# A branch that is never taken on GpSimd, and fifteen small loads among the large ones

## The chip, the cores and the metric

The kernel runs on one NeuronCore of a Trainium2 chip. A core has a matrix engine (TensorE, PE in the profile), a vector engine (VectorE, DVE), a scalar engine (ScalarE, ACT), a general engine (GpSimd, POOL) and a synchronisation engine (SyncE, SP). Each has its own instruction stream; they meet through semaphores. Sixteen DMA engines move data between device memory (HBM) and the on-chip memory SBUF, which has 128 partitions; TensorE writes into PSUM. SP and ACT put transfers on queues of their own (q1 and q10 in the profile's rows), and the engines' instructions are brought in by a further queue (q8). The metric is device time in microseconds of one execution.

## The reference

The reference is one step of a decoder for one token: grouped-query attention over a cached context, a SwiGLU feed-forward block, and a scalar gate that mixes the two.

```python
def reference(A_x, A_k_cache, A_v_cache, A_wq, A_wo, B_x, B_w_gate, B_w_up, B_w_down, gate_w):
    x = A_x                                                   # [1, 1, 512]
    g = sigmoid((x * gate_w).sum(-1, keepdims=True))
    q = (x @ A_wq)  -> 32 heads of 128                        # wq [512, 4096]
    k, v: caches [1, 8, 32768, 128], each used by 4 heads
    p = softmax(q @ k^T * 128 ** -0.5)
    a = (p @ v) -> [1, 1, 4096] @ A_wo                        # wo [4096, 512]
    b = (silu(x @ B_w_gate) * (x @ B_w_up)) @ B_w_down        # F = 1792
    return g * a + (1 - g) * b
```

All tensors are bf16. The two caches are 64 MiB each, so nearly everything that is moved is K and V: 8 groups of 8 MiB of K and 8 MiB of V.

## The kernel before, in words

**Loads.** SP issues nearly all loads, in this order: wq (4 MiB), w_gate and w_up (1.75 MiB each), then K of group 0 in two halves of 4 MiB, K of group 1 in two halves, V of group 0, and from then on in turn K of group g and V of group g-1, each as one load of 8 MiB in which each of the 128 partitions receives 64 KiB. Last come V of group 7, w_down, two small remainders of w_down, and wo in five pieces. `load_k` and `load_v` do the issuing. SBUF holds five pages of 32 KiB per partition (`page`), so SP waits before most of these loads until a page is free: a K load waits until half of the preceding group's K has been transposed (`sem_fill`, L311; for the second half of group 1, L320), a V load until the V products of an earlier group are done (`sem_v_free`, L335), V of group 0 until the feed-forward projections are done (`sem_pe_h`). SP runs in program order, so what stands behind a waiting load waits with it.

**TensorE.** Its program is one loop of two turns with two tests, so that the code of the end stands ahead of the code of the start. The start (`emit_start`) makes an identity matrix from a row of indices (`r_row`, L476), turns x into a column (L482), computes the q projection (L497) when wq has landed, brings q into place (L522), and computes the gate and up projections (L535) when those weights have landed, followed by small steps (L553, L566). Then a loop over the 8 groups: K is transposed on TensorE in 16 units (L371) into PSUM, VectorE copies each unit to SBUF (`ktT`, L765), TensorE multiplies it by q (L383). The maximum, the exponentials (ACT, L633) and the products with V (L440) of a group follow, the V products one group later than the K work. The end (`emit_end`) adds the last group's V products, the down projection (L235) and the product with wo (L235, L246).

**GpSimd.** POOL's program is short. It fills `ones_f` and `ones_bf` (L278, L279), builds `r_row` by doubling (L280 to L290: seven additions and one negation), and then only passes on semaphore counts of the K loads, and late in the kernel clears the small tile for the remainders of w_down (L301). TensorE's very first matmul waits for `ones_f`, `ones_bf` and `r_row`; VectorE's work at the start and all of TensorE's program stand behind that matmul.

**Tiles.** `pad` is a tile that nothing uses; its size comes from `PAD`. It stands ahead of `page` in SBUF, so its size moves `page` and the tiles behind it.

Of the kernel before, what the change touches and what calls it, by code (L numbers as in the profile page):

```python
# [8 lines left out]
BF16 = mybir.dt.bfloat16  # L9
# [3 lines left out]
def bass_gated_mix__gqa_block_cached__swiglu_ffn__decode_kernel(  # L13
# [61 lines left out]
    NPG = 5  # L75
    assert G % 2 == 0
    PAD = 768

    XH, XE, XQ, FX = 2, 4, 4, 4
    XP = XE * XQ  # L80
# [6 lines left out]
    with ExitStack() as es:  # L87
        def S_(name):
            return es.enter_context(nc.semaphore(name))
# [10 lines left out]
        sem_ld_wd = S_("s_ld_wd")  # L100
        sem_ld_wx = S_("s_ld_wx")
        sem_wz = S_("s_wz")
        sem_ones = S_("s_ones")
        sem_dc = S_("s_dc")
        sem_pz = S_("s_pz")
# [42 lines left out]
        def T(name, shape, dt):  # L148
            return es.enter_context(nc.sbuf_tensor(name, shape, dt))
# [6 lines left out]
        ones_f = T("ones_f", [128, 128], FP32)  # L156
# [11 lines left out]
        tX = T("tX", [XS, FX], BF16)  # L168
        pad = T("pad", [128, PAD // 2], BF16)
        page = T("page", [128, NPG, PAGE], BF16)  # L170
# [14 lines left out]
        O2a = T("O2a", [128, WOJ], BF16)  # L185
        O2 = T("O2", [128, WOJ], BF16)
        res_row = T("res_row", [128, 128], BF16)

        def P(name, shape, dt):
            return es.enter_context(nc.psum_tensor(name, shape, dt))  # L190
# [78 lines left out]
        def emit_store(eng, half, rows):  # L269
            eng.dma_start(  # L270
                out[0, 0, 256 * half : 256 * (half + 1)].rearrange("(c n) -> c n", c=2),
                rows[31 + 64 * half : 33 + 64 * half, :],
            ).then_inc(sem_out, 16)

        with nc.Block("main") as block:
            @block.gpsimd
            def _(pool):
                pool.memset(ones_f[:, :], 1.0).then_inc(sem_ones, 1)  # L278
                pool.memset(ones_bf[:, :], 1.0).then_inc(sem_ones, 1)  # L279
                pool.memset(r_row[:, 0, 0:1], 0.0).then_inc(sem_r, 1)  # L280
                n, k = 1, 1
                while n < 128:
                    pool.wait_ge(sem_r, k)
                    pool.tensor_scalar(
                        r_row[:, 0, n : 2 * n], r_row[:, 0, 0:n], float(n), None, op0=ALU.add
                    ).then_inc(sem_r, 1)
                    n *= 2
                    k += 1
                pool.wait_ge(sem_r, k)
                pool.tensor_scalar(  # L290
                    r_row[:, 1, :], r_row[:, 0, :], -1.0, None, op0=ALU.mult
                ).then_inc(sem_r, 1)
                for g in range(1, G):
                    pool.wait_ge(sem_k[1], 16 * g)
                    if g > 1:
                        pool.wait_ge(sem_k[0], 16 * (g + 1))
                    else:
                        pool.wait_ge(sem_k1, 16)
                    pool.sem_inc(sem_k[1], 16)
                pool.wait_ge(sem_fill, UPG * G)  # L300
                pool.memset(wz, 0.0).then_inc(sem_wz, 1)  # L301

            @block.sync
            def _(sp):
                def load_k(g):
                    lo = PG_A if g % 2 else PG_B
                    dst = page[:, lo : lo + NB, :].rearrange("p b (r d) -> p b r d", d=DH)
                    src = A_k_cache[0, g, :, :].rearrange("(p b r) d -> p b r d", b=NB, r=R)
                    if g > 1:
                        sp.wait_ge(sem_fill, UPG * (g - 1) + UPP)  # L310
                        sp.dma_start(  # L311
                            dst.rearrange("p b r d -> p (b r d)"),
                            src.rearrange("p b r d -> p (b r d)"),
                        ).then_inc(sem_k[0], 16)
                        return
                    for b in range(NB):
                        first = lo + b == PG_B
                        if g and first:
                            sp.wait_ge(sem_fill, UPP)
                        sp.dma_start(dst[:, b, :, :], src[:, b, :, :]).then_inc(  # L320
                            sem_k[0] if first else sem_k1 if g else sem_k[1], 16
                        )

                def load_v(g):
                    src = A_v_cache[0, g, :, :].rearrange("(p b r) d -> p b r d", b=NB, r=R)
                    if g == G - 1:
                        lo, sem = PG_L, sem_vl
                        sp.wait_ge(sem_fill, UPG * g + UPP)
                    else:
                        lo, sem = PG_V, sem_v  # L330
                        if g:
                            sp.wait_ge(sem_v_free, STEP * (g + 1))
                        else:
                            sp.wait_ge(sem_pe_h, 1)
                    sp.dma_start(  # L335
                        page[:, lo : lo + NB, :].rearrange("p b n -> p (b n)"),
                        src.rearrange("p b r d -> p (b r d)"),
                    ).then_inc(sem, 16)

                sp.dma_start(wq_v, A_wq.rearrange("(p c) n -> p c n", c=KC)).then_inc(sem_q, 16)  # L340
                for w, src in enumerate((B_w_gate, B_w_up)):
                    sp.dma_start(
                        wgu[:, w, :, :], src.rearrange("(p c) f -> p c f", c=KC)
                    ).then_inc(sem_f, 16)
                load_k(0)
                for g in range(1, G):
                    load_k(g)
                    load_v(g - 1)
                load_v(G - 1)
                sp.dma_start(  # L350
                    wd[:, :, :], B_w_down[0:FR, :].rearrange("(p j) n -> p j n", j=FM)
                ).then_inc(sem_ld_wd, 16)
                sp.wait_ge(sem_wz, 1)
                rest = B_w_down[FR:F, :].rearrange(
                    "(h q e i) n -> h e q (i n)", h=XH, q=XQ, e=XE
                )
                for h in range(XH):
                    sp.dma_start(wx[h], rest[h]).then_inc(sem_ld_wx, 16)
                sp.wait_ge(sem_v_free, STEP * G)
                src = A_wo.rearrange("(p j) n -> p j n", j=WOJ)  # L360
                for k, s in enumerate(sem_wo):
                    a, b = WO_CUTS[k], WO_CUTS[k + 1]
                    sp.dma_start(wo_v[:, a:b, :], src[:, a:b, :]).then_inc(s, 16)  # L363
# [445 lines left out]
        pe, act, dve, sp = nc.tensor, nc.scalar, nc.vector, nc.sync  # L809
# [9 lines left out]
        for half, eng in enumerate((sp, act)):  # L819
            eng.wait_ge(sem_dve_row, 1)  # L820
            emit_store(eng, half, res_row)
        sp.wait_ge(sem_out, 32)


# [26 lines left out]
```

## Time and profile before

| | |
|---|---|
| median of 3 runs | 349.12 us (348.97 to 349.3) |
| the profiled execution | 349.16 us |
| its span, first to last instruction | 347.8 us |
| moved from HBM | 148.11 MB, 426 GB/s over the span |
| busy share of PE, DVE, ACT, POOL | 75%, 54%, 10%, 1% |
| mean granted TensorE clock | 0.851 |
| POOL instructions | 16, 4.6 us in all |

Engines: PE is TensorE's matrix work and PEld its weight loads, DVE VectorE, ACT ScalarE, POOL GpSimd, SP SyncE; a trailing q (SPq, ACTq) is an engine's instruction sequencer. A row of the timeline gives start, duration, engine, line, operation, what is written and read, how often, and in brackets the idle time before and what ended it. A row of the DMA queues gives queue, packets, MB and the time of its packets as a share of 16 engines over the span or the window asked for. A row "DMA packets" counts the packets of a window and how many were smaller than 512 B, 2 KB and 8 KB (each count holds the ones before). A row of the stages gives start and end, then for PE, PEld, DVE, ACT and POOL the busy time and the number of instructions, the granted clock, the DMA share and GB/s.

### The profile page before, as it was taken

The page shows a single profiled execution, that of the slowest core. Times are in us where ns is not written, and L with a number is a line of the kernel's source. Part 1 is how long each engine was busy: PE and PEld are TensorE (multiplying, and loading weights), DVE is VectorE, ACT ScalarE, POOL GpSimd, SP SyncE. Part 2 cuts the span into 40 slices and gives each one's busy share as a digit, 9 for nine tenths or more (in the row PEclk, how much of TensorE's full clock was granted, in tenths as well). Part 3 has the DMA queues.
Part 4 walks back from the last instruction along what each step waited for, and adds up shares of the span by engine and source line. Part 5 has one row for each costly group of instructions (what it writes and reads, how often), then busy time and mean ns, then how long its engine had stood idle before and what let it go on. Part 6 is the DMA issues. An engine that isn't in the chain of part 4 may idle for free.

```text
span 347.8 us, 8869 instructions
## 1 busy us (share of the span) xinstructions
PE 260.8 (75%) x3925; PEld 220.6 (63%) x3925; DVE 186.6 (54%) x232; ACT 33.4 (10%) x143; POOL 4.6 (1%) x16
## 2 busy tenths in 40 slices
PE   1354995999749982999459982999469972999475
PEld 1124994998449941997259942996269842996232
DVE  3144995698119931697129921895149820895101
ACT  1002000300130003000300003000400012000400
POOL 3000000000000000000000000000000000002000
PEclk9996999699659987699959985898869985898669
DMA  8999999999999999999999999999999999999996
GB/s 322 419 459 426 420 422 458 469 414 437 414 430 475 415 437 415 437 467 415 437 407 445 467 414 437 407 452 460 414 437 407 452 460 415 437 407 452 406 418 261
DMA packets 3946, 148.21 MB, mean 426 GB/s; under 512 B 450, under 2 KB 580, under 8 KB 868
## 3 DMA queue, kind: packets, MB, share of 16 engines
q1 hardware_dynamic: 3932, 148.11, 98.7%
q8 instruction: 6, 0.10, 0.1%
q10 hardware_dynamic: 8, 0.00, 0.0%
HBM read 148.11 MB, written 0.00 MB: 426 GB/s over the span
## 4 chain that ended last, share of the span: by engine, by line
DMA 64%; PE 33%; DVE 2%; issue 1%; SPq 1%; ACT 0%; DVEq 0%
DMA page<-in_A_k_cache_dram 52%; PE pst L371 24%; DMA page<-in_B_w_up_dram 6%; DMA page<-in_A_wo_dram 6%; PE ps_sc L383 5%; PE ps_o L440 2%; PE pst L535 1%; DVE ktT L722 1%; DVE ktT L765 0%; SPq L363 0%; PE ps_m L553 0%; PE ps_m L566 0%; DVE ktT L712 0%; DVE ktT L710 0%; PE ps_sc L246 0%
## 5 line engine op out<-in xcount | busy, mean ns | idle before, releaser
L765 DVE COPY ktT<-pst 128x2048 bf16<-128x2048 bf16 x128 | 153.3, 1221 | 64.6 <-PE pst L371 60.4
L371 PE MATMUL pst<-ident_f,page 128*128 128x128 f32 x1024 | 147.2, 299 | 39.5 <-DMA page<-in_A_k_cache_dram 38.2
L371 PEld LDWEIGHTS pst<-ident_f,page 128*128 128x128 f32 x1024 | 126.0, 154 | 43.9 <-DMA page<-in_A_k_cache_dram 38.8
L383 PE MATMUL ps_sc<-qcur,ktT 128*128 128x8 bf16 x2048 | 64.1, 166 | 6.3 <-DVE ktT L765 6.3
L383 PEld LDWEIGHTS ps_sc<-qcur,ktT 128*128 128x128 bf16 x2048 | 63.8, 97 | 8.0 <-DVE ktT L765 7.1
L440 PE MATMUL ps_o<-page,ET 128*16 128x512 bf16 x512 | 39.4, 477 | 5.5 <-DMA page<-in_A_v_cache_dram 5.5
L440 PEld LDWEIGHTS ps_o<-page,ET 128*16 128x16 bf16 x512 | 15.0, 107 | 26.1 <-issue 18.8
L633 ACT ACTIVATE ET<-ps_sc,nbias 128x128 bf16 x64 | 23.9, 555 | 49.9 <-DVE nbias L791 49.9
L626 ACT ACTIVATE acc<-ps_o 128x512 f32<-128x512 f32 x8 | 4.8, 597 | 223.8 <-PE ps_o L440 218.9
L783 DVE TENSOR_REDUCE gm<-ps_m 4x1 f32<-4x128 f32 x8 | 2.2, 279 | 40.6 <-PE ps_m L420 40.6
L633 ACT ACTIVATION_READ_ACCUMULATOR ET<-ps_sc,nbias 128x1 f32 x64 | 18.3, 285 | 0.0
L773 DVE TENSOR_REDUCE pmaxf<-ps_sc 128x4 f32<-128x512 f32 x16 | 11.0, 686 | 8.4 <-PE ps_sc L383 8.4
L497 PE MATMUL pst<-page,xT 128*1 128x512 bf16 x32 | 3.6, 627 | 8.9 <-DMA page<-in_A_wq_dram 8.9
L461 PE MATMUL ps_m<-sel,acc 128*128 128x4 f32 x64 | 8.4, 255 | 1.8 <-ACT acc L626 1.6
L461 PEld LDWEIGHTS ps_m<-sel,acc 128*128 128x128 f32 x64 | 7.7, 191 | 2.5 <-ACT acc L626 2.2
L424 PE MATMUL ps_m<-diag,ones_f 4*128 4x4 f32 x16 | 3.8, 306 | 6.8 <-DVE diag L787 6.8
L424 PEld LDWEIGHTS ps_m<-diag,ones_f 4*128 4x128 f32 x16 | 3.3, 259 | 8.4 <-issue 8.4
L750 DVE RECIPROCAL rS<-ps_m 128x4 f32<-128x4 f32 x9 | 1.6, 182 | 12.2 <-PE ps_m L461 12.2
L497 PEld LDWEIGHTS pst<-page,xT 128*1 128x1 bf16 x32 | 0.9, 115 | 10.7 <-issue 10.7
L685 DVE CAST ktT<-pst 128x1024 bf16<-128x1024 f32 x2 | 2.4, 1220 | 8.2 <-PE pst L497 8.2
L452 PEld LDWEIGHTS ps_m<-esum,ones_f 128*128 128x128 f32 x32 | 4.2, 190 | 3.5 <-issue 3.5
L301 POOL MEMSET page<- 48x2048 bf16 x1 | 1.8, 1798 | 311.7 <-PE pst L371 311.7
(76 smaller groups left out, 54.6 us busy)
## 6 DMA issues: line engine op xcount, KB each, us to landing
page<-in_A_k_cache_dram SPq DMA_DIRECT2D x4, 4096.0 KB, 34.9
page<-in_A_wq_dram SPq DMA_DIRECT2D x1, 4096.0 KB, 13.4
page<-in_A_wo_dram SPq DMA_DIRECT2D x1, 2048.0 KB, 17.4
page<-in_B_w_gate_dram SPq DMA_DIRECT2D x1, 1792.0 KB, 17.2
page<-in_B_w_up_dram SPq DMA_DIRECT2D x1, 1792.0 KB, 21.0
wd<-in_B_w_down_dram SPq DMA_DIRECT2D x1, 1664.0 KB, 30.3
page<-in_A_wo_dram SPq DMA_DIRECT2D x1, 1152.0 KB, 19.8
page<-in_A_wo_dram SPq DMA_DIRECT2D x1, 512.0 KB, 20.6
```

The costliest lines, as they stand in the source:

```text
L371: ins = pe.transpose(pst[u % NST][:, k * 128 : (k + 1) * 128], kv[:, n * 128 : (n + 1) * 128], ident_f[:, :],)
L383: ins = pe.matmul(ps_sc[b][:, col : col + 2 * HPG], kt[:, k, e, :], qcur[:, e, :], start=(e == 0), stop=(e == 1),)
L424: pe.matmul(ps_m[:, M_B0 : M_B0 + HPG], ones_f[0:HPG, :], diag[:, :], start=True, stop=True,).then_inc(sem_b, STEP)
L440: ins = pe.matmul(ps_o[32 * c : 32 * c + RQ * HPG, :], ET[:, n : n + RQ, :].rearrange("p n h -> p (n h)"), v[:, k * RQ : (k + 1) * RQ, :], ...
L452: pe.matmul(ps_m[:, M_S0 : M_S0 + HPG], ones_f[:, :], esum[:, b, :], start=(b == 0), stop=(b == NB - 1),)
L461: ins = pe.matmul(ps_m[:, M_P0 : M_P0 + HPG], acc[:, q, :], sel4[:, q * HPG : (q + 1) * HPG], start=(q == 0), stop=(q == RQ - 1),)
L497: ins = pe.matmul(pst[0][32 * k : 32 * k + 1, t * QN : (t + 1) * QN], xT[:, c : c + 1], wq_v[:, c, n : n + QN], start=(c == 0), stop=(c == ...
L535: ins = pe.matmul(pst[1][32 * k : 32 * k + 1, w * 512 : w * 512 + FS], xT[:, c : c + 1], wgu[:, w, c, k * FS : (k + 1) * FS], start=(c == ...
L626: act.activation(part, ps_o[:, :], ACT.Copy).then_inc(sem_acc, STEP)
L633: act.activation(ET[:, b * R : (b + 1) * R, h], sc[:, h, bass.ds(bank, R)], ACT.Exp, bias=nbias[:, h : h + 1], scale=SCALE, accum_out=esum ...
L765: dve.tensor_copy(ktT[:, n % NKT, :], pst[n % NST][:, :].bitcast(BF16)).then_inc(sem_cp, 1)
L773: dve.tensor_reduce(pmaxf[:, b, :], sc, AX.X, ALU.max).then_inc(sem_d, 1)
```

## The change

Three things are added.

- POOL's program begins with a loop of two turns. Inside are two nested tests, `turn > 0` and `turn < 1`, which are never true together, and inside these 1536 memsets of `ones_f`. They are part of the program and never run.
- `mark`, a tile of 16 partitions by 15 by 64 bf16 elements at the end of SBUF's tiles, receives fifteen loads from the first rows of wq: 15 rows of 128 bytes, then 14, down to 1 row. One is issued by SP after each K load from group 1 on and after each V load. Nobody reads the tile. SP waits at the very end until all fifteen have landed.
- `PAD` becomes 1536, which is the count of memsets and also makes the unused tile `pad` 1536 instead of 768 bytes per partition.

```diff
     PAD = 768
+    MARKS = list(range(15, 0, -1))
+    PAD = 1536
...
+        sem_mark = S_("s_mark")
...
         res_row = T("res_row", [128, 128], BF16)
+        mark = T("mark", [16, len(MARKS), 64], BF16)
...
             @block.gpsimd
             def _(pool):
+                with pool.Fori(0, 2, 1) as turn:
+                    with pool.If(turn > 0):
+                        with pool.If(turn < 1):
+                            for _ in range(PAD):
+                                pool.memset(ones_f[:, :], 1.0)
                 pool.memset(ones_f[:, :], 1.0).then_inc(sem_ones, 1)
...
+                marks = list(enumerate(MARKS))
+
+                def load_mark():
+                    if marks:
+                        m, n = marks.pop(0)
+                        sp.dma_start(mark[0:n, m, :], A_wq[0:n, 0:64]).then_inc(sem_mark, 16)
+
...
                 for g in range(1, G):
                     load_k(g)
+                    load_mark()
                     load_v(g - 1)
+                    load_mark()
                 load_v(G - 1)
+                load_mark()
+                assert not marks
...
             emit_store(eng, half, res_row)
+        sp.wait_ge(sem_mark, 16 * len(MARKS))
         sp.wait_ge(sem_out, 32)
```

## The prediction

> **What bounds the kernel now.** I read the page first: shares, queues, chain.
>
> ```profile
> span 347.8 us, 8869 instructions
> DMA packets 3946, 148.21 MB, mean 426 GB/s; under 512 B 450, under 2 KB 580, under 8 KB 868
> q1 hardware_dynamic: 3932, 148.11, 98.7%
> q8 instruction: 6, 0.10, 0.1%
> DMA 64%; PE 33%; DVE 2%; issue 1%; SPq 1%; ACT 0%; DVEq 0%
> ```
>
> SP's queue (q1) keeps the 16 DMA engines 98.7% busy. PE's third of the chain is no bound: the chain alternates between a K load and the transposes that free a page for the next one, while other loads are still queued. So the time is the bytes over the transfer rate, and an edit costs something if it gives the slowest DMA engine more work or lets the engines run dry.
>
> Which engine is slowest shows in narrow windows on the DMA packets. Every large load ends with 16 packets under 512 B, one per engine. I take five loads, each with two windows, early and late finishers, and the windows that count q8, the instruction packets.
>
> ```profile
> DMA packets 48, 0.49 MB, mean 378 GB/s; under 512 B 15, under 2 KB 15, under 8 KB 15
> DMA packets 21, 0.29 MB, mean 410 GB/s; under 512 B 1, under 2 KB 1, under 8 KB 1
> ...
> DMA packets 30, 0.52 MB, mean 437 GB/s; under 512 B 14, under 2 KB 14, under 8 KB 14
> DMA packets 18, 0.52 MB, mean 374 GB/s; under 512 B 2, under 2 KB 2, under 8 KB 2
> ...
> DMA packets 29, 0.52 MB, mean 437 GB/s; under 512 B 13, under 2 KB 13, under 8 KB 13
> DMA packets 19, 0.51 MB, mean 363 GB/s; under 512 B 3, under 2 KB 3, under 8 KB 3
> ...
> DMA packets 27, 0.88 MB, mean 681 GB/s; under 512 B 11, under 2 KB 11, under 8 KB 11
> DMA packets 14, 0.59 MB, mean 347 GB/s; under 512 B 5, under 2 KB 5, under 8 KB 5
> ...
> DMA packets 20, 0.66 MB, mean 1092 GB/s; under 512 B 10, under 2 KB 10, under 8 KB 10
> DMA packets 12, 0.39 MB, mean 562 GB/s; under 512 B 6, under 2 KB 6, under 8 KB 6
> ```
>
> The windows are 12 to 13.3 and 13.3 to 14 us; 39.8 to 41 and 41 to 42.4; 49.4 to 50.6 and 50.6 to 52; 59 to 60.3 and 60.3 to 62; 310.6 to 311.2 and 311.9 to 312.6. Late engines: 1, 2, 3, 5, 6, and 6 still at 312 us.
>
> ```profile
> q8 instruction: 1, 0.02, 11.0%
> ...
> q8 instruction: 1, 0.02, 0.6%
> ...
> q8 instruction: 1, 0.02, 0.7%
> ...
> q8 instruction: 2, 0.03, 1.2%
> ...
> q8 instruction: 1, 0.02, 0.3%
> ```
>
> These are 4.5 to 5 us, 30 to 40, 40 to 49, 49 to 59 and 59 to 78: instruction packets so far 1, 2, 3, 5, 6, the same counts. I read it so: each 16 KB instruction packet goes through one DMA engine, each of PE's six through another one, and that engine stays behind for good, because its own queue never empties. The packet takes 11.0% of 16 x 0.5 us = 0.88 us; the lag is 312.25 - 310.9 = 1.35 us between the middles of the two windows (0.7 to 2.0 by their edges). I take 1.3 us. So six late engines set the end and the other ten have 1.3 us to spare.
>
> **The memsets.** None runs, so their execution costs nothing. POOL now has to jump over them (turn 0, outer test), back to the loop's head, and over them again (turn 1, inner test). Between 30 and 78 us PE drew five blocks of 16 KB for about 1,030 instructions of its loop's code (448 transposes and matmuls for K, both page variants counted, and 64 for V, each with its weight load): an estimate of some 80 bytes each, a little high if the last block reaches past the loop. 1536 memsets are then some 120 KB, seven such blocks, and the jump's target lies far outside the block or two that PE drew ahead. No row shows a far jump on POOL. Fetches: none at the low end, 14 at the high end (all seven blocks read in both turns); I take three to six, one or two blocks for each jump. [...]
>
> What they cost has two parts. First, DMA time: a packet on an engine that is already late moves the end by 1.3 us; on one of the ten others it is free. Dropped on 16 engines at random, three packets miss all six late ones with 10/16 x 9/15 x 8/14 = 0.21, six with 0.03; but blocks may be dealt in an order that stays clear of PE's, or not be fetched, so I keep a third for no hit. One hit: +1.3 us.
>
> Second, POOL's start slips. Rows of the start, from the timelines of POOL, DVE, ACT, PE and SP:
>
> ```profile
> 0.74 0.20 POOL L278 MEMSET ones_f<- 128x128 f32 x1 [0.29 <-POOLq L836]
> 3.46 0.53 POOL L290 TENSOR_SCALAR r_row<-r_row 1x128 f32<-1x128 f32 x1
> ...
> 6.11 0.15 DVE L675 CAST xT<-ps_m 128x4 bf16<-128x4 f32 x1
> 8.36 0.68 DVE L678 TENSOR_TENSOR gp_row<-x_row,gw_row 1x512 f32<-1x512 bf16 x1 [2.09 <-DMA gw_row<-in_gate_w_dram]
> ...
> 0.74 0.53 ACTq L612 DMA_DIRECT2D x_row<-in_A_x_dram  x1
> 1.30 0.22 ACTq L613 DMA_DIRECT2D gw_row<-in_gate_w_dram  x1
> ...
> 4.04 0.79 PE L476 MATMUL ps_sc<-ones_f,r_row 1*128 1x128 f32 x2 [4.04 <-POOL r_row L290]
> 14.28 3.58 PE L497 MATMUL pst<-page,xT 128*1 128x512 bf16 x32 [8.92 <-DMA page<-in_A_wq_dram]
> 20.42 0.57 PE L522 MATMUL ps_o<-ident,ktT 128*128 128x4 bf16 x16 [2.04 <-DVE ktT L685]
> 22.68 3.05 PE L535 MATMUL pst<-page,xT 128*1 128x448 bf16 x32 [1.69 <-DMA page<-in_B_w_up_dram]
> ...
> 0.74 0.41 SPq L340 DMA_DIRECT2D page<-in_A_wq_dram  x1
> 2.13 42.14 SPq L320 DMA_DIRECT2D page<-in_A_k_cache_dram  x4
> ...
> q10 hardware_dynamic: 2, 0.00, 0.2%
> ```
>
> POOL's r_row opens PE's program, and behind that first matmul wait the transposition of x, both projections and the first K fills. Cover: xT is ready at 6.11 + 0.15 = 6.26 and PE then waits for wq until 14.28: 8.0 us. L535 waits 1.7 us for w_up. A later slip moves the fills, and with them SP's issue of the fourth K half (end of the L320 row, 44.27 us, begun at 43.95). A transfer starts about 1.1 us after its issue begins (wq: issue 0.74, first packets between 1.5 and 2 us), so at 45.05; the late engines finish what is queued after 50.6 us, which leaves 5.5 us, and the others, from 49.4, have 4.4 plus the 1.3 that they may lose. Cover in all: 8.0 + 1.7 + 5.5 = 15.2 us; past it each us of slip costs one.
>
> The slip: the nearest rows are single small loads on ACT's queue. x_row, issued before the large transfers run, has its packets before 2 us (last row: window 0 to 2 us), about 1.3 us after issue; gw_row, issued by 1.52, is waited for until 8.36, 6.8 us, behind wq's packets. One jump like x_row and two like gw_row: 1.3 + 6.8 + 6.8 = 14.9 us, just inside the cover: cost nothing. Ends: 0, and 3 x 6.8 = 20.4 us, which is 5.2 us over.
>
> **The marks.** Fifteen loads with 120 rows of 128 bytes. SP's issue: about 0.41 us each (the L340 row), ahead of V(g-1), the next K and wd, issued while the transfers before them still run (over 5 us of them at 44.27 us, above); that queue hides it, and without it 15 x 0.41 = 6.2 us would show. POOL's and ACT's queues are not passed. The closing wait is on loads that were finished long before the output. Bytes: nothing. Packets, from the windows 345 to 345.5 and 345.5 to 346 us:
>
> ```profile
> DMA packets 67, 0.06 MB, mean 121 GB/s; under 512 B 12, under 2 KB 63, under 8 KB 67
> q1 hardware_dynamic: 67, 0.06, 34.9%
> ...
> DMA packets 2, 0.00 MB, mean 0 GB/s; under 512 B 2, under 2 KB 2, under 8 KB 2
> q1 hardware_dynamic: 2, 0.00, 0.2%
> ```
>
> Completion packets: 0.2% of 8 us over 2, about 8 ns. Mostly 1 KB packets: 34.9% of 8 us over 67, about 42 ns. A row of 128 bytes lies between; with its completion 16 to 50 ns, so 0.24 to 0.75 us on an engine that serves all fifteen loads, half of it on a middling one. I take 0.2 us, near the low end, as 128 bytes are nearer to the completion packet; a saving is excluded, since nothing is taken away. [...]
>
> **The tiles.** pad grows by 768 bytes per partition, so page and all behind it move; mark comes last. Wherever in page the loads of before go, the rate is the same (436 and 432 GB/s over 100 us each):
>
> ```profile
> 100.00:200.00 100.00, 82.93 (x1267) 75.01 (x1268) 61.88 (x67) 7.18 (x34) 0.00 (x0) 0.86 1.01 436
> 200.00:300.00 100.00, 74.93 (x1107) 63.66 (x1104) 50.02 (x63) 10.77 (x51) 0.00 (x0) 0.81 1.00 432
> ```
>
> I take 0; by the difference of these rows (0.9%) the ends are -3 and +3 us.
>
> **Sum.** The profiled execution took 349.16 us, 0.04 above the median of 349.12. 349.12 + 1.3 (one hit) + 0 (slip covered) + 0.2 (marks) = 350.6 us.
>
> **Rivals.** (a) No hit: POOL's packets go to engines with time to spare, or the skipped code is never fetched. For: ten of 16 are free, and PE's six never doubled. Against: three to six draws. 349.12 + 0.0 to 0.4, so 349.3. (b) POOL is late past its cover: the deciding point is a slip of 15.2 us, and 14.9 is near it. For: gw_row's 6.8 us. Against: wq's packets end at 14 us, and shorter ones follow. 20.4 us of slip gives 349.12 + 5.2 + 0.2 = 354.5; a slip of 17 gives 351.1. [...] (c) The marks are dear: all rows on one engine, 120 x 16 to 50 ns = 1.9 to 6 us there, 350 to 355. Against: each load's 16 completions come from as many engines. (d) Faster: page's new offset speeds up the writes into it. It decides from 0.2% of rate, 0.7 us; 0.5% gives 347.4 us. Against: the equal rates above.
>
> **How the numbers follow.** One hit or two (350.3 to 352.2) 0.36; (a) 0.31; (b) 0.20; (c) 0.07; (d) 0.06. A measurement of this kernel can tell about 0.2%, 0.7 us, from no change. Faster is (d), 0.06; same is (a), 0.31; slower is the rest, 0.63. The likeliest gives 350.6. The range reaches down to (a), 348.9, and up to 353.0, which takes in both hits and half of (b); what is left out is (d) and the far ends of (b) and (c), about 0.17.
>
> **What will show it.** q8 with 9 to 12 packets instead of 6, three or more before 20 us; r_row's last step at 10 to 20 us instead of 3.46; DMA share still 1.0 between 45 and 55 us if the slip is covered, a dip if (b). At 311 us a third group of completions, 1.3 us behind the six, shows a hit; two groups only, with the time unchanged, show (a). I am wrong if q8 stays at 6, or if the marks' packets last far longer than 50 ns.

## The result, and the profile after

The changed kernel takes 350.43 us (median of 7 runs, 349.85 to 350.58) against 349.10 us before (7 runs, 348.97 to 349.30): 1.3 us more, a ratio of 1.0033 with a 95% interval of 1.0023 to 1.0043. The time lies 0.2 us below the forecast of 350.6 us. The profiled execution is the fastest of the seven, 349.85 us with a span of 348.5 us, so its traces show 0.7 us of the difference, not all of it; a second profile of the same program, taken later (`after_again`), took 350.22 us.

From the page of the changed kernel, the packets and queues:

```profile
span 348.5 us, 8894 instructions
DMA packets 4188, 148.25 MB, mean 425 GB/s; under 512 B 690, under 2 KB 820, under 8 KB 1108
q1 hardware_dynamic: 4172, 148.13, 98.6%
q8 instruction: 6, 0.10, 0.1%
q14 instruction: 2, 0.02, 0.0%
```

240 more packets under 512 B than before: 120 rows and 120 completions. So the fifteen loads of 15 to 1 rows ended with one completion for each row; 16 for each load would be 240 completions alone. For the load of 15 rows the window 58.4 to 62 us, with the end of a K load, shows it alone: 46 packets, 15 rows, its 15 completions and the K load's 16. PE's six instruction packets are unchanged. Two more, 0.02 MB together, came on a queue of their own, q14. POOL's start, from its timeline, and those two packets, from windows 1.5 to 3 and 7 to 8 us on the DMA queues:

```profile
4.29 0.21 POOL L287 MEMSET ones_f<- 128x128 f32 x1 [3.84 <-issue]
7.00 0.53 POOL L299 TENSOR_SCALAR r_row<-r_row 1x128 f32<-1x128 f32 x1
...
q14 instruction: 1, 0.01, 2.9%
...
q14 instruction: 1, 0.01, 1.9%
```

POOL starts at 4.29 instead of 0.74 us, a slip of 3.55 us. By its share of 2.9% of 24 us (16 engines times 1.5 us) the first packet took 0.70 us, and by 1.9% of 16 us the second 0.30 us, 8 KB at 27 GB/s. The first stands in POOL's wait. The second runs at 7 to 8 us, when POOL already does its own work, so nobody waits for it. PE takes up the slip before wq lands, as its timeline shows: q projection at 14.34 us instead of 14.28, gate projection at 22.73 instead of 22.68.

```profile
14.34 3.58 PE L517 MATMUL pst<-page,xT 128*1 128x512 bf16 x32 [5.43 <-DMA page<-in_A_wq_dram]
22.73 3.11 PE L555 MATMUL pst<-page,xT 128*1 128x448 bf16 x32 [1.68 <-DMA page<-in_B_w_up_dram]
```

So the time was added elsewhere. The next windows follow the loads to the end. First 331.9 to 332.6 us, right after the landing of the last V load, before and after:

```profile
DMA packets 26, 0.35 MB, mean 494 GB/s; under 512 B 0, under 2 KB 0, under 8 KB 0
```
```profile
DMA packets 23, 0.31 MB, mean 437 GB/s; under 512 B 0, under 2 KB 0, under 8 KB 0
```

In both all completions are in by 331.9 us: up to here the last engine of the changed kernel is no later than before. Then 335.75 to 337.5 us, after w_down and its remainder (the remainder being the two last loads issued ahead of wo), before and after:

```profile
DMA packets 47, 0.77 MB, mean 440 GB/s; under 512 B 0, under 2 KB 0, under 8 KB 0
```
```profile
DMA packets 49, 0.75 MB, mean 428 GB/s; under 512 B 1, under 2 KB 1, under 8 KB 4
```

Before, every engine has finished w_down by 335.75 us. After, one has not: it still moves rows of 4 KB, which only the remainder has at this place, and finishes late. The output store, from SP's timeline, comes 0.68 us later (before, after):

```profile
346.51 0.29 SPq L270 DMA_DIRECT2D out_dram<-res_row  x1
```
```profile
347.19 0.28 SPq L274 DMA_DIRECT2D out_dram<-res_row  x1
```

How many engines carry the remainder is to be read from the completions between 332.6 and 337.5 us: 24 before, 16 for w_down itself and 8 for two remainder loads, so four engines each.

```profile
DMA packets 186, 2.09 MB, mean 427 GB/s; under 512 B 24, under 2 KB 24, under 8 KB 56
```

32 rows of 4 KB (56 - 24) over four engines are eight rows each, if both loads use the same four. The packet times of the trace say that they do: four rows, a completion, four rows and a completion follow on each other without a gap, for instance from 334.44 to 335.69 us. At the steady rate of 436 GB/s over sixteen engines, 27.25 GB/s for one, these 32 KB take 1.2 us: about the lag of an instruction packet. The four engines that were not late before this point are therefore almost as late as the six behind it, and have hardly anything to spare: the last of these rows ends at 335.69 us, and the last completion of w_down on the six comes at 335.66.

### The profile page after: what moved, and what is told of

Same layout as the page of the kernel before. It is cut to its first block, busy times and chain, and to the rows that moved or that the text cites. A ratio compares the mean times of both kernels' runs of the same rounds, so it can differ in the third digit from the quotient of the medians.

```text
span 348.5 us, 8894 instructions
## 1 busy us (share of the span) xinstructions
PE 260.8 (75%) x3925; PEld 220.2 (63%) x3925; DVE 186.5 (54%) x232; ACT 33.4 (10%) x143; POOL 4.6 (1%) x16
## 3 DMA queue, kind: packets, MB, share of 16 engines
q1 hardware_dynamic: 4172, 148.13, 98.6%
## 4 chain that ended last, share of the span: by engine, by line
DMA 64%; PE 32%; DVE 2%; issue 1%; SPq 1%; ACT 0%; DVEq 0%
DMA page<-in_A_k_cache_dram 52%; PE pst L391 24%; DMA page<-in_A_wo_dram 6%; DMA page<-in_B_w_up_dram 6%; PE ps_sc L403 5%; PE ps_o L460 2%; PE pst L555 1%; DVE ktT L742 1%; SPq L383 0%; DVE ktT L785 0%; PE ps_m L573 0%; PE ps_m L586 0%; DVE ktT L732 0%; DVE ktT L730 0%; ACT ktT L639 0%
## 5 line engine op out<-in xcount | busy, mean ns | idle before, releaser
L460 PEld LDWEIGHTS ps_o<-page,ET 128*16 128x16 bf16 x512 | 14.9, 107 | 26.2 <-issue 19.3
L496 PE MATMUL ps_sc<-ones_f,r_row 1*128 1x128 f32 x2 | 0.8, 496 | 7.6 <-POOL r_row L299 7.6
(76 smaller groups left out, 54.9 us busy)
```

The costliest lines, as they stand in the source:

```text
L460: ins = pe.matmul(ps_o[32 * c : 32 * c + RQ * HPG, :], ET[:, n : n + RQ, :].rearrange("p n h -> p (n h)"), v[:, k * RQ : (k + 1) * RQ, :], ...
```

## The experiments

Two theories. A is the prediction's: six late engines set the end, and POOL's instruction packets fall on one of these. B came from the windows above: the four engines with the remainder set the end after the change; the small loads and POOL's packet fall on these. The expectations call these four the lowest; no row numbers an engine, so the word is a name of the author's. That loads of 4 rows fall on them is a guess here, which `low4` tries. Medians are over 5 to 12 runs, compared with runs of the kernel before that were taken alongside (349.27 us for the first four experiments, 349.20 us for the rest).

**The parts alone.** The branch without the small loads and with the old tile:

```diff
+                with pool.Fori(0, 2, 1) as turn:
+                    with pool.If(turn > 0):
+                        with pool.If(turn < 1):
+                            for _ in range(1536):
+                                pool.memset(ones_f[:, :], 1.0)
```

> The kernel before plus the branch with its 1536 memsets; no small loads, unused tile as before. Theory A (the prediction's: the end is set by six engines that each carried one of PE's instruction packets, and POOL's packets fall on one of these): 350.4 us, all of the change's 1.3 us. Theory B (the end after the change is set by the four engines that carry the remainder of w_down, and both a POOL packet and the small loads fall on these): a part of it, 0.4 to 0.7 us, 349.5 to 349.8. POOL's first own memset at 4.3 us instead of 0.74, without effect on the K fills, in both.

349.51 us, ratio 1.0009 (1.0000 to 1.0018): 0.24 us. Both q14 packets are there, and POOL starts at 4.31 us. One completion stands behind 335.75 us; the store is issued at 346.77 us.

```profile
DMA packets 49, 0.79 MB, mean 449 GB/s; under 512 B 1, under 2 KB 1, under 8 KB 1
...
346.77 0.29 SPq L273 DMA_DIRECT2D out_dram<-res_row  x1
```

A's full 1.3 us is excluded. The interval, 0.0 to 0.6 us, still reaches into B's 0.4 to 0.7, though the median lies below it. Where POOL's packets fell shows at the place that the prediction named, the completions of a V load in the windows 310.6 to 311.2, 311.2 to 311.9 and 311.9 to 312.6 us. The kernel before has 10, 0 and 6 of them; this run:

```profile
DMA packets 18, 0.59 MB, mean 983 GB/s; under 512 B 9, under 2 KB 9, under 8 KB 9
DMA packets 2, 0.07 MB, mean 94 GB/s; under 512 B 1, under 2 KB 1, under 8 KB 1
DMA packets 12, 0.39 MB, mean 562 GB/s; under 512 B 6, under 2 KB 6, under 8 KB 6
```

The late ones are still six, and no completion follows up to 313.9 us. There is no third group behind the six, so POOL's packets did not fall on a late engine, as A had it. One of the ten early engines has fallen back, but `slip2` below, without the branch, has one in the middle window too, so this profile alone does not say that it was POOL's. The small loads alone, without the branch:

> The kernel before plus the fifteen small loads; no branch. Theory A: 0.2 us or less, since the late six get only some of the packets: 349.1 to 349.3. Theory B: the small loads weigh most on the lowest engines, 15 pairs of packets of 13 + 9 ns, 0.33 us, on top of the remainder of w_down: 0.2 to 0.4 us, 349.3 to 349.5. If they cost more than the time of their packets, more than that.

349.82 us, 0.55 us more, ratio 1.0013 (1.0004 to 1.0022). The windows 331.9 to 332.6 and 335.75 to 337.5 us, and the store: two completions are late already behind the last V load, six behind w_down.

```profile
DMA packets 28, 0.35 MB, mean 494 GB/s; under 512 B 2, under 2 KB 2, under 8 KB 2
...
DMA packets 64, 0.82 MB, mean 466 GB/s; under 512 B 6, under 2 KB 6, under 8 KB 17
...
347.15 0.28 SPq L274 DMA_DIRECT2D out_dram<-res_row  x1
```

By the median this is more than the range of either theory; the interval, 0.1 to 0.8 us, reaches into both. The unused tile alone:

```diff
-    PAD = 768
+    PAD = 1536
```

> The kernel before with the unused tile at 1536 instead of 768 bytes per partition. Both theories: no change, 349.1 us. The rival that the place of the page tile matters: a change of over 0.3 us in either direction.

349.15 us, ratio 1.0000 (0.9991 to 1.0009): nothing.

> The changed kernel once more, for a second profile. Both theories: 350.4 us. Theory A: the late engines' lag at the last V load is larger than before by 0.3 us or more. Theory B: it is the same as before, and the extra time appears between the last V load's and w_down's landings.

350.39 us, ratio 1.0034 (1.0021 to 1.0048). In this profile both groups are late: two completions behind the last V load, nine behind w_down, with nine rows of 4 KB (18 - 9) still moving there; the store is issued at 347.56 us.

```profile
DMA packets 24, 0.29 MB, mean 418 GB/s; under 512 B 2, under 2 KB 2, under 8 KB 2
...
DMA packets 64, 0.79 MB, mean 452 GB/s; under 512 B 9, under 2 KB 9, under 8 KB 18
...
347.56 0.28 SPq L274 DMA_DIRECT2D out_dram<-res_row  x1
```

Here B's expectation, the same lag at the last V load, missed, and A's came true: two completions behind 331.9 us, none before. But `marks_only`, without any packet of POOL's, shows the same two. So the small loads push the late engines back as well, which neither theory's price for them contains.

By the medians the parts do not add up: 0.24 + 0.55 = 0.79, against 1.12 to 1.33 for the whole. The gap of 0.3 to 0.5 us is not clear of the noise of three medians, each known to some 0.3 us. It would be expected if both fall on the same engines and these had a little to spare before. With a spare time s, a cost b of the branch and m of the small loads on the engine, b - s = 0.24, m - s = 0.55 and b + m - s = 1.2 give s = 0.4, b = 0.65, m = 0.95 us. That is an estimate from these medians, and not itself measured.

**Load on the four engines alone.** The kernel before with four loads of 4 rows after V of group 3, nothing else:

```diff
+                    if g == 4:
+                        sp.dma_start(mark[0:4, :], A_wq[0:4, 0:2816]).then_inc(sem_mark, 16)
...
+                        sp.dma_start(mark[12:16, :], A_wq[12:16, 0:2816]).then_inc(sem_mark, 16)
```

> The kernel before plus four loads of 4 rows of 5,632 bytes after V of group 3: four packets of 0.21 us, 0.84 us, on each of the four lowest engines, which no PE packet has delayed. Theory A: these engines have 1.3 us to spare, so no change: 349.1 to 349.3. Theory B: they finish w_down's remainder only 0.1 us before the late six, so 0.6 to 0.9 us more: 349.8 to 350.2.

350.36 us, 1.16 us more, ratio 1.0031 (1.0019 to 1.0043). Theory A's spare 1.3 us does not exist. 90 KB on four engines cost as much as the whole change. In the trace the 16 packets took 4.27 us together, 1.07 us for each engine. The windows 332.6 to 337.5 and 335.75 to 337.5 us:

```profile
DMA packets 194, 2.16 MB, mean 441 GB/s; under 512 B 24, under 2 KB 24, under 8 KB 56
...
DMA packets 74, 0.78 MB, mean 447 GB/s; under 512 B 9, under 2 KB 9, under 8 KB 32
```

Nine completions are late and 23 of the remainder's 32 rows (32 - 9) are still being moved in the second window, where the kernel before moves none: the remainder's engines are the last, and with eight rows to an engine at least three of the four are late.

Single packets of the traces show that such an engine sets the end. Times in us:

| run | last row of the remainder ends | last completion of wo's loads |
|---|---|---|
| kernel before | 335.69 | 345.54 |
| `branch_only` | 335.91 | 345.76 |
| `marks_only` | 336.29 | 346.14 |
| changed kernel | 336.33 | 346.18 |
| `after_again` | 336.76 | 346.61 |
| `low4` | 337.04 | 346.89 |

The distance is 9.85 us in all six, so the engine that ends the remainder last also ends wo last, in the kernel before as well. In `pad_only` and `slip2`, which cost nothing by their medians, it is 9.87 and 10.10 us, so there another engine is last: before the change the two groups end together.

**Relief of the four engines.** First by splitting the remainder over sixteen engines, in the kernel before and in the changed one:

```diff
-    XH, XE, XQ, FX = 2, 4, 4, 4
+    XH, XE, XQ, FX = 2, 1, 16, 4
```

> The kernel before, with the rows of w_down's remainder split 1 x 16 instead of 4 x 4, so that each of the two remainder loads runs on sixteen engines instead of four. Each remainder row takes about 0.16 us on its engine. Theory A and B alike: the six late engines get two such rows each, 0.3 us more: 349.3 to 349.6 us. It is the base for the next run.

350.54 us, 1.34 us more than before where 0.1 to 0.4 were expected, ratio 1.0045 (1.0032 to 1.0058). The completions are 48, so the loads did run on sixteen engines, but the transfer rate fell to 299 and 330 GB/s in the two stages 334 to 336 and 336 to 338 us, with the engines counted as busy. Windows of completions of this run; then the two stages of the kernel before; then of this run:

```profile
DMA packets 186, 1.70 MB, mean 346 GB/s; under 512 B 48, under 2 KB 48, under 8 KB 80
```
```profile
334.00:336.00 2.00, 2.00 (x24) 0.66 (x20) 0.00 (x0) 0.00 (x0) 0.00 (x0) 0.50 1.08 456
336.00:338.00 2.00, 2.00 (x35) 1.00 (x28) 0.00 (x0) 0.15 (x1) 0.00 (x0) 0.98 1.01 434
```
```profile
334.00:336.00 2.00, 2.00 (x24) 0.79 (x20) 0.00 (x0) 0.00 (x0) 0.00 (x0) 0.50 1.00 299
336.00:338.00 2.00, 2.00 (x24) 0.73 (x20) 0.00 (x0) 0.00 (x0) 0.00 (x0) 0.58 1.04 330
```

> The changed kernel with the remainder of w_down on sixteen engines. Theory A (POOL's packets fall on late engines): the 1.3 us stay, so 1.3 us above the same edit to the kernel before: 350.6 to 350.9. Theory B (the four engines with the remainder are the last): they are relieved of 1.2 us, the small loads and POOL's packet disappear in the spare time of the early engines, and only what the small loads put on the six late ones is left: 0.1 to 0.5 us above the same edit to the kernel before, 349.4 to 350.0.

351.05 us, ratio to the kernel before 1.0050 (1.0037 to 1.0063), 0.51 us above the same edit to the kernel before. The size of the difference is B's, but the edit slows the whole tail, so it is no clean test. The clean one leaves the two loads out (the rows count as zero and the output lacks them):

```diff
-                for h in range(XH):
-                    sp.dma_start(wx[h], rest[h]).then_inc(sem_ld_wx, 16)
...
-                    pe.wait_ge(sem_ld_wx, 16 * XH)
+                    pe.wait_ge(sem_wz, 1)
```

> The kernel before without the two loads of w_down's remainder; these 128 rows of w_down count as zero, so that part of the feed-forward output is left out. Theory A and B alike: the six late engines carry none of it and still set the end: 349.1 to 349.3 us. It is the base for the next run.

349.11 us, ratio 0.9998 (0.9990 to 1.0007): without the remainder the end stays, so the six late engines held it too.

> The changed kernel without the two loads of w_down's remainder (the same part of the feed-forward output is left out). Theory A: POOL's packets and the small loads weigh on the six late engines, so all of the change's 1.2 us stays: 350.3 to 350.5. Theory B: the four lowest engines, relieved of 1.25 us, are no longer last; what stays is what the small loads put on the late six: 0.1 to 0.5 us above the same edit to the kernel before, 349.3 to 349.7.

349.61 us, 0.50 us above the same edit to the kernel before, instead of 1.2 to 1.3. Some 0.7 to 0.8 us of the change went with the remainder, as B has it; A would have kept all. What stays is at the upper end of B's 0.1 to 0.5 us for the small loads on the late engines. The windows 335.75 to 337.5 us of the two runs, the kernel before first, hold two and one completions, but the two profiled executions took 349.38 and 349.37 us, so they do not show the 0.50 us of the medians:

```profile
DMA packets 49, 0.77 MB, mean 440 GB/s; under 512 B 2, under 2 KB 2, under 8 KB 2
```
```profile
DMA packets 48, 0.77 MB, mean 440 GB/s; under 512 B 1, under 2 KB 1, under 8 KB 1
```

**POOL's slip.** Two runs hold POOL back with memsets of w_down's tile ahead of its own work:

```diff
+                for k in range(2):     # 3 in the second run
+                    pool.memset(wd[:, :, :], 0.0).then_inc(sem_slip, 1)
+                    pool.wait_ge(sem_slip, k + 1)
```

> The kernel before, with GpSimd's start held back by two memsets of w_down's tile, an estimated 5.8 us each by the 1.8 us of the 48 x 2048 memset. Cover of 15.2 us right: no change, 349.1 to 349.4 us, with PE's q projection late by some 4 us and the gate projection by 2. Cover wrong (8.0 us, the wait for wq alone): 3 to 4 us more.

349.29 us, ratio 1.0013 (1.0000 to 1.0026), 0.09 us by the medians; two of the twelve runs took 351.3 us, which the profile, at 349.10 us, does not explain. The slip is 12.14 - 0.74 = 11.4 us, and the q projection starts 3.5 us late:

```profile
0.74 11.35 POOL L280 MEMSET wd<- 128x6656 bf16 x2 [0.29 <-POOLq L841]
12.14 0.20 POOL L282 MEMSET ones_f<- 128x128 f32 x1
...
17.76 3.38 PE L502 MATMUL pst<-page,xT 128*1 128x512 bf16 x32 [1.01 <-issue]
```

> GpSimd's start held back by three memsets of w_down's tile, 17.1 us by the 11.35 us that two took. The prediction's cover of 15.2 us: 1.9 us over, so 351.0 to 351.3 us. If the other engines' queues smooth it out: less than 0.5 us.

354.15 us, ratio 1.0150 (1.0127 to 1.0172): 5.0 us for a slip of 17.85 - 0.74 = 17.1, where 1.9 was expected. The start of the gate projection, SP's row of the K loads, the DMA's stage 45 to 60 us in this run, and the same stage before:

```profile
30.10 3.15 PE L540 MATMUL pst<-page,xT 128*1 128x448 bf16 x32
...
2.13 50.56 SPq L324 DMA_DIRECT2D page<-in_A_k_cache_dram  x4
...
45.00:60.00 15.00, 14.99 (x255) 14.52 (x255) 13.83 (x13) 0.00 (x0) 0.00 (x0) 1.00 0.77 315
```
```profile
45.00:60.00 15.00, 11.56 (x220) 10.57 (x217) 11.18 (x13) 0.00 (x0) 0.00 (x0) 0.99 1.08 461
```

The gate projection starts 30.10 - 22.68 = 7.4 us late, exactly the slip less the first two covers (17.1 - 8.0 - 1.7). From there the third cover, 5.5 us, leaves 1.9 us, but more was lost: (461 - 315) GB/s x 15 us = 2.2 MB, 5.0 us at 436 GB/s. The fourth K half was issued by 2.13 + 50.56 = 52.69 us instead of 44.27, 8.4 us late and not 7.4, so 2.9 us past the cover; why stays open. No packet of data starts from 50.5 to 53.3 us. The windows 53.3 to 54.9 and 54.9 to 56.1 us hold the next 32:

```profile
DMA packets 16, 0.52 MB, mean 328 GB/s; under 512 B 0, under 2 KB 0, under 8 KB 0
q1 hardware_dynamic: 16, 0.52, 113.3%
...
DMA packets 16, 0.52 MB, mean 437 GB/s; under 512 B 0, under 2 KB 0, under 8 KB 0
q1 hardware_dynamic: 16, 0.52, 100.9%
```

The first sixteen took 113.3% of 1.6 us, 1.8 us each, the next sixteen 100.9% of 1.2, 1.2 us each: 0.6 us more were lost at the restart, and then the rate was full again. This profiled execution took 356.15 us, 2.0 us above its median; the stage accounts for 5.0 of its 7 us, and where the rest went is open.

The branch with 16 memsets instead of 1536:

> The kernel before plus the same branch with 16 memsets instead of 1536; no small loads, unused tile as before. If the distance of the jump is what costs: no instruction packets for GpSimd, its first memset before 1.5 us instead of 4.3, and no change of the time, 349.1 to 349.3. If the branch itself costs: as with 1536, 349.5.

349.16 us, ratio 1.0001 (0.9992 to 1.0009). No q14 packet, and POOL's first memset at 1.70 us:

```profile
1.70 0.20 POOL L286 MEMSET ones_f<- 128x128 f32 x1 [1.25 <-issue]
```

So of the slip of 3.55 us the branch with 16 memsets makes 1.70 - 0.74 = 0.96, and 1536 memsets in their place 4.29 - 1.70 = 2.6 us more.

## Why the prediction came out

The time, the sign and the general mechanism held: the kernel is bound by its slowest DMA engine (in six runs wo's last completion stands 9.85 us behind the last row of the remainder, early or late), and what the change costs it costs by putting packets on the engines that end last. The single steps held less well. That the sum came within 0.2 us is luck: the branch was priced 1.1 us too high, the small loads 0.35 us too low, and the rest is what the two cost together beyond their single prices.

- **PE's six packets make six late engines that set the end.** Confirmed as far as the last V load and by the run without the remainder, which keeps the time (349.11 us). Incomplete after that: in the kernel before, an engine with the remainder ends as late as they do (335.69 and 335.66 us).
- **"The other ten have 1.3 us to spare."** This step failed. It was read at 312 us, before the last loads. Four of the ten carry 1.2 us of the remainder of w_down, and the load on these four alone cost 1.16 us. The completions of the tail, 24 where loads on all sixteen engines would leave 48, would have shown it before.
- **Fetches: three to six of 16 KB, one hit, +1.3 us.** Two came, of 8 KB, and none fell on a late engine: no profile with the branch has a group behind the six at 311 us. The branch alone cost 0.24 us. The term was too large by 1.1 us, and its mechanism, a hit on a late engine, did not occur. PE's rows show blocks of 16 KB (0.10 MB for six), POOL's 8 KB (0.02 MB for two). That each of three jumps waits for fetches was an assumption, and no run shows it: one packet, of 0.70 us, stands in POOL's wait, which is 2.6 us longer with 1536 memsets than with 16.
- **Slip 14.9 us, covered.** The term adds three waits for fetches, 1.3 + 6.8 + 6.8 us, that no run shows; the slip was 3.55 us, with one packet in it. Its size was wrong, its cost of zero was right, and the cover of at least 11.4 us holds.
- **Cover 15.2 us, then one for one.** The first two parts, 8.0 and 1.7 us, are confirmed by `slip3` to 0.1 us and by `slip2`, whose gate projection started 24.20 - 22.68 = 1.5 us late instead of 1.7, to 0.2 us. Beyond the cover the price was too low: 5.0 instead of 1.9 us, of which 1.0 came with the later issue and 0.6 with the slow first packets.
- **Marks 0.2 us.** They cost 0.55 us, inside the ends of 0.24 to 0.75, nearer the high one. The packets were as short as taken: in the traces a row took 13 ns and its completion 9, so 0.33 us for fifteen on one engine. The mistake was to take half of that for a middling engine, where the engines of the remainder, among the last, are the ones that fell behind: in `marks_only` 11 of their 32 rows (17 - 6) still move after 335.75 us, none before. How many of the 120 rows each engine took no row names, and what the loads cost beyond 0.33 us is not explained. Rival (c), at 1.9 to 6 us, begins at 351 us and not at 350.
- **Tile 0.** Confirmed, 1.0000 (0.9991 to 1.0009).
- **Sum.** 1.3 + 0.2 was forecast. The runs show 0.24 for the branch, 0.55 for the small loads and a rest of 0.3 to 0.5, not clear of the noise, which fits two costs on the same engine and which a sum of separate terms could not have held.
- **The signs.** q8 stayed at 6 packets, which the prediction named as a sign of being wrong: POOL's packets came on q14, and two instead of three to six. r_row's last step began at 7.00 us, not at 10 to 20. At 311 us there is no third group behind the six, the sign of rival (a), no hit; yet the time did not stay as (a) had it.

Which engine POOL's packets fell on is known only in part. At 311 us one of the ten early engines stands 0.4 to 0.7 us behind the other nine in the four profiles that have the branch and the small loads (`after_nowx` and `after_x16` are two of them), and by at most 0.25 us in the six that have neither POOL's packets nor small loads. The last row of the remainder ends on a single engine, 0.6 and 0.8 us behind the other three, in the two profiles of the changed kernel, 0.4 us behind in `branch_only`, and 0.05 to 0.35 us behind in the runs without POOL's packets. So they fell on one of the remainder's engines in the changed kernel and probably in `branch_only`. Why on these, and why the small loads cost more than their packets, stays open.

## What to carry to other kernels

In a kernel bound by transfers, account for each DMA engine separately and down to the last load: average share and total bytes hide which engine is last (98.7% busy before, 98.6% after), while completions counted in narrow windows show it (10 early and 6 late at 311 us). Here the two remainder loads ended with 8 completions together where one large load has 16, and 90 KB in loads of 4 rows cost 1.16 us. A small load or a fetch of instructions is to be priced by what it adds to the engine that ends last. The branch and the small loads cost 0.24 and 0.55 us alone and 1.12 to 1.33 together, and a slip 1.9 us past its cover cost 5.0 us.

## What had not been expected

- Splitting the remainder from four engines to sixteen made the tail slower by 1.34 us, with the rate down from 456 to 299 GB/s at the same bytes. In the trace the remainder's rows took 0.16 us as before, mostly, but wo's 16 KB packets 0.72 us on average instead of 0.61, up to 1.42. The cause was not tried; each of the two loads goes to the same 16 partitions as before.
- Small loads cost more than their bytes: the four loads of `low4`, 0.83 us for each engine at 27.25 GB/s, took 1.07 us of each engine's time in the trace and cost 1.16 us at the end.
- A slip that should have run past its cover by 1.9 us cost 5.0 us. The queue ran dry, and its first packets after the gap took 1.8 instead of 1.2 us.
- POOL's instruction packets are half as large as PE's (0.02 MB for two, against 0.10 MB for six) and came on another queue.
